# Block transposes on VectorE and DMAs in place of TensorE transposes for z, x1 and the attention's output

## The chip, the cores and the metric

The kernel runs on one core of one Trainium2 chip. The metric is the device time of one execution in microseconds (us). TensorE (PE) multiplies, VectorE (DVE), ScalarE (ACT) and GpSimd (POOL) do the element-wise work, and SyncE (SP) issues all the DMAs. Each engine works through its own queue in the order in which the program hands it instructions; engines wait for one another through semaphores.

## The reference

Two branches read the same normalised input, and their sum is added to x. There are S = 2048 tokens with D = 576 features; all data are float32.

```python
x = A_x
xn = _layernorm(x, axis=-1)
return x + _A_ref(xn, A_wqkv, A_wo) + _B_ref(xn, B_w1, B_w2, B_w3, B_w4)
# _A_ref: qkv = xn @ wqkv; 32 heads of 18; each token attends to 8 tokens, 2 apart, behind it
#         softmax over the 8; o = attn . v; return o @ wo
# _B_ref: z = layernorm(xn); h = gelu(z @ w1); four quarters of h shifted by +1, -1, +2, -2 tokens
#         x1 = xn + shifted @ w2
#         return x1 + gelu(layernorm(x1) @ w3) @ w4        # w3: 576 x 4608, w4: 4608 x 576
```

## The kernel before

Every product is made of float32r halves: an operand is split into a rounded part ("hi") and the rest ("lo"), and the pairs hi.hi, hi.lo and lo.hi are added up in PSUM. 576 features are four chunks of 128 and one tail of 64; in the fifth chunk the hi part of the tail lies in partitions 0 to 63 and its lo part in 64 to 127, so one matmul treats both. With that there are 14 matmuls per product (`PAIRS`).

A matmul wants the features in the partitions, while the norms want the tokens there. So a normalised token tile (128 tokens x 576) is transposed: `transposes` (L97) lets TensorE transpose four 128x128 blocks into a PSUM buffer, and for every second tile a fifth block that holds the 64-wide tails of two tiles side by side (`tail_half`, `pair_tail`). ScalarE then copies the hi part out of PSUM (L107, L110) and VectorE subtracts it for the lo part (L111, L114). The result goes into a block of 512 tokens, `xt[128, 9, 512]`, in a ring of two buffers (`ring_block`).

The stages, one after the other on TensorE:

- **QKV** (to L348): 16 token tiles; `x_stage` normalises and transposes xn two tiles ahead, `q_half` multiplies it by half of wqkv, and `spill` writes the result to DRAM.
- **Mix** (L422 on): four blocks b of 512 tokens. For each, `mix_tile` (14 matmuls with 512 columns into one of `psa`'s two PSUM buffers, two gelus on ScalarE, one subtraction on VectorE) for m = 0, 1, 2, then `mix_rem` (9 matmuls; its result goes through eight DMAs L400/L401 and a list of later steps, `todo`), then `mix_tile` 3. `z_norm` and `z_prep` prepare the z tiles of the next block, one after each of the first four. Between them the four or five pieces of w2 are loaded (`load_w2`, two buffers; piece 4 has eight DMAs, L370) and split.
- **W2** (L481 on): 16 token tiles; `mm_tok` writes one of `psb`'s three PSUM buffers, VectorE adds it to Y and takes the statistics for the next norm; from tile 6 on, `n_norm` and `n_prep` prepare x1 tile t - 6.
- **MLP units** (L697 on): 72 units (c, b), c = 0 to 17 and b = 0 to 3. A unit has two `up` (14 matmuls with 512 columns, two gelus, one subtraction) and then the four `down` of the unit before it (12 matmuls each, one addition to Y on VectorE). `LATE` names the x1 tiles 8 to 15, which are prepared in units 0 to 2. From unit 3 on, VectorE gets the attention in small pieces between its other work (`bg`); the attention's DMAs are on SP as well, and its result goes to DRAM (`od`). Weights w3 and w4 are loaded by `load_f` into `rawf`, which has two buffers; so is wo (`load_wo`, L660) in the last four units.
- **Output** (L750 on): 16 token tiles of o, loaded from `od` (`load_o`), transposed by `prep_o` three tiles ahead, multiplied by wo and added to Y; VectorE also adds x again (L695). Then the tile is stored.

The schedule is written by hand: the order of the calls is the order in each engine's queue. A tile of a pool is reused when whatever used its memory before has been released.

Of the kernel before, what the change touches and what calls it, by code (L numbers as in the profile page):

```python
# [8 lines left out]
F32 = mybir.dt.float32  # L9
# [20 lines left out]
HF = D // 2  # L30
# [15 lines left out]
def fused_block(ctx, tc, x, wqkv, wo, w1, w2, w3, w4, out):  # L46
# [25 lines left out]
    def tail_half(t):  # L72
        if t % 2 == 0:
            ztail[t // 2] = base.tile([128, 128], F32, name="ztail", bufs=2)
        return ztail[t // 2][:, t % 2 * 64:t % 2 * 64 + 64]

    def norm_z(dst, kind, t):
        norm(dst, Y[:, t, :512], kind, t)
        norm(tail_half(t), Y[:, t, 512:], kind, t)
# [36 lines left out]

    def split_w(dst_hi, dst_lo, raw):
        act.copy(dst_hi, raw)  # L118
        dve.tensor_tensor(dst_lo, raw, dst_hi.bitcast(F32), op=ALU.subtract)
# [20 lines left out]
    zp = {}  # L140

    def z_norm(t):
        zp[t] = w1pool.tile([128, 512], F32, name="z", bufs=2)
        norm_z(zp[t], 1, t)

    def z_prep(t):
        xt = ring_block(("z", t // 4))
        transposes(zp[t], pair_tail(ztail[t // 2], xt, t), xt, (t % 4) * 128)
# [177 lines left out]
    for t in range(4, NT):  # L326
        for h in range(2):
            q_half(t, h)
            if h == 0:
# [6 lines left out]
                if t >= NT - 2:  # L336
                    z_prep(2 * (t - NT + 2) + 1)
                    z_norm(2 * (t - NT + 2) + 3)
                if t in (5, 6):
                    split_w1(t - 5)  # L340
            else:
                if t == NT - 4:
                    z_norm(0)
                    z_norm(1)
                if NT - 3 <= t < NT - 1:
                    z_prep(2 * (t - NT + 3))
                    z_norm(2 * (t - NT + 3) + 2)
# [13 lines left out]
    pool.memset(T4[:, S:S + 4].bitcast(F32), 0.0)  # L361

    def load_w2(k):
        r = mpool.tile([128, D], F32, name="rz", tag="rz", bufs=2)
# [11 lines left out]
    def mix_tile(b, m):  # L376
        xt = xring[("z", b)]
        ps = psa.tile([128, 512], F32, name="p1", tag="a")
        for i, (a, w) in enumerate(PAIRS):
            pe.matmul(ps, W1[:, w, m * 128:(m + 1) * 128], xt[:, a, :],  # L380
                      start=i == 0, stop=i == len(PAIRS) - 1)
        g32 = mpool.tile([128, 512], F32, name="g32", bufs=1)
# [8 lines left out]
    def mix_rem(b):  # L391
        xt = xring[("z", b)]
        ps = psa.tile([128, 512], F32, name="p1", tag="a")
        for a in range(9):
            pe.matmul(ps, W1R[:, a if a < 5 else a - 5, :], xt[:, a, :], start=a == 0, stop=a == 8)  # L395
        u = mpool.tile([128, 512], F32, name="u", bufs=2)
        v = mpool.tile([128, 512], F32, name="v", bufs=2)
# [24 lines left out]
    for b in range(NB):  # L422
        for i, m in enumerate((0, 1, 2, 4, 3)):
            nz = 4 * (b + 1) + i
# [44 lines left out]
    def n_norm(t, zpool):  # L469
        zp[t] = zpool.tile([128, D], F32, name="rz", tag="rz", bufs=2)[:, :512]  # L470
        norm_z(zp[t], 2, t)

    def n_prep(t):
        xt = x1n.get(t // 4)
        if xt is None:
            xt = x1n[t // 4] = ring_block(("n", t // 4))
        transposes(zp[t], pair_tail(ztail[t // 2], xt, t), xt, (t % 4) * 128)
# [3 lines left out]
    for t in range(NT):  # L481
        ps = psb.tile([128, 2, 512], F32, name="ps", tag="b")
        if 6 <= t < 14:
            n_norm(t - 6, mpool)
# [12 lines left out]
        if t in (1, 3):  # L497
# [14 lines left out]
    hp = ctx.enter_context(tc.tile_pool(name="hp", bufs=2, reuse_waits="tile"))  # L512

# [98 lines left out]
    def up(c, b, i):  # L612
        f = c * C + i
        ps = psa.tile([128, 512], F32, name="p1", tag="a")
        for n, (a, w) in enumerate(PAIRS):
            pe.matmul(ps, W3[f][:, w, :], x1n[b][:, a, :], start=n == 0, stop=n == len(PAIRS) - 1)  # L616
# [28 lines left out]
    LATE = {(0, 0): (8, 9), (0, 1): (10, 11), (1, 0): (12,), (1, 1): (13,), (2, 0): (14,), (2, 1): (15,)}  # L645
    Wo = None
    oT = {}
# [27 lines left out]
    def load_o(t):  # L675
        if t % 2 == 0 and t < NT:
# [119 lines left out]
```

## Time and profile before

| what | us |
|---|---|
| median of 3 runs | 1322.92 |
| lowest and highest run | 1322.52, 1323.04 |
| the profiled execution | 1322.94 |
| span of its instructions | 1321.2 |
| TensorE, matmuls busy | 1312.1 (99%) |
| VectorE busy | 921.9 (70%) |
| ScalarE busy | 348.2 (26%) |
| mean granted TensorE clock | 1.0 |

In the profiled execution the mix begins at 197 us, the W2 stage at 264, the units at about 328 and the output at 1250. Busy time of an engine is a mean over stages, and a matmul's duration overlaps the next one's; so the chain of work that ended last, and the starts in the timeline, say more of TensorE's pace than its busy share. In rows of the groups, "out<-in" are the program's names, then come the shapes, the count, the busy time and the mean duration in ns, and at the end the idle time before the group with what released it. Rows with "SPq" are SP's queue; their time includes waits when several are merged.

### The profile page before, as it was taken

The numbers are of one execution on the slowest core, as the hardware profiler recorded it, in microseconds if no ns is written. First come the engines' busy times: TensorE is split into PE (matmuls) and PEld (weight loads), VectorE is DVE, ScalarE is ACT, GpSimd is POOL, SyncE is SP. The second block draws the span as 40 slices with busy tenths as digits, with TensorE's granted clock in tenths as the row PEclk, the third lists the DMA queues.
The fourth block names the chain that finished last, engine by engine and source line by source line (L and its number), as shares of the span: only waits on it lengthen the run. The fifth ranks groups of instructions, "written<-read, shape, count | busy, mean of one in ns | idle before, by whom it ended". The sixth has DMA issues, their size and how long they took to land.

```text
span 1321.2 us, 18855 instructions
## 1 busy us (share of the span) xinstructions
PE 1312.1 (99%) x7894; PEld 1208.0 (91%) x7894; DVE 921.9 (70%) x1332; ACT 348.2 (26%) x633; POOL 35.2 (3%) x92
## 2 busy tenths in 40 slices
PE   8999999999999999999999999999999999999998
PEld 8999998899899999999999999999999999999998
DVE  6443326687676778878868868878877886884454
ACT  4322225411423222222122222223213223122111
POOL 2010100011000000000000000000000000000000
PEclk9999999999999999999999999999999999999999
DMA  7644322020112021221221220220320200212164
GB/s 211 152 107 108 98 68 69 18 82 28 59 30 80 20 71 39 71 71 39 71 71 29 80 71 20 90 71 20 90 71 19 82 28 20 71 42 95 46 192 140
DMA packets 120325, 93.76 MB, mean 71 GB/s; under 512 B 73504, under 2 KB 100000, under 8 KB 120240
## 3 DMA queue, kind: packets, MB, share of 16 engines
q1 hardware_dynamic: 120240, 92.56, 23.9%
q8 instruction: 62, 1.02, 0.3%
q14 instruction: 23, 0.19, 0.0%
HBM read 67.83 MB, written 23.66 MB: 69 GB/s over the span
## 4 chain that ended last, share of the span: by engine, by line
PE 96%; DVE 2%; ACT 1%; SPq 1%; issue 1%; DMA 0%; POOL 0%; DVEq 0%; ACTq 0%; POOLq 0%
PE ps L636 34%; PE p L616 34%; PE ps L133 18%; PE ps L230 3%; PE p L380 3%; PE ps L102 2%; PE p L272 0%; PE p L395 0%; PE p L764 0%; DVE bn L88 0%; PE ps L105 0%; ACT xt L107 0%; DVE xt L111 0%; SPq L370 0%; DVE xt L114 0%
## 5 line engine op out<-in xcount | busy, mean ns | idle before, releaser
L636 PE MATMUL ps<-W,hi 128*128 128x288 f32 x2304 | 397.9, 294 | 0.5 <-DVE oT L114 0.5
L636 PEld LDWEIGHTS ps<-W,hi 128*128 128x128 f32 x2304 | 339.5, 188 | 6.1 <-PE ps L102 0.7
L620 ACT ACTIVATE hi<-p 128x512 fp32r<-128x512 f32 x144 | 86.2, 599 | 619.3 <-PE p L616 619.3
L636 PE MATMUL ps<-W,lo 128*128 128x288 f32 x1152 | 245.3, 294 | 0.0
L616 PE MATMUL p<-xt,W 128*128 128x512 f32 x1008 | 235.4, 390 | 0.0
L616 PE MATMUL p<-x1n,W 128*128 128x512 f32 x1008 | 234.9, 389 | 0.0
L622 DVE TENSOR_TENSOR lo<-g,hi 128x512 fp32r<-128x512 f32 x144 | 99.7, 692 | 193.2 <-ACT g L621 193.2
L639 DVE TENSOR_TENSOR Y<-ps,Y 128x576 f32<-128x576 f32 x288 | 212.8, 751 | 16.3 <-PE ps L636 16.1
L616 PEld LDWEIGHTS p<-x1n,W 128*128 128x128 f32 x1008 | 187.2, 188 | 36.8
L616 PEld LDWEIGHTS p<-xt,W 128*128 128x128 f32 x1008 | 187.1, 188 | 36.9
L636 PEld LDWEIGHTS ps<-W,lo 128*128 128x128 f32 x1152 | 185.4, 187 | 0.0
L133 PE MATMUL ps<-WQ,xt 128*128 128x432 f32 x672 | 135.3, 360 | 0.0
L133 PEld LDWEIGHTS ps<-WQ,xt 128*128 128x128 f32 x672 | 125.2, 188 | 5.2
L111 DVE TENSOR_TENSOR xt<-ps,xt 128x512 fp32r<-128x512 f32 x40 | 27.6, 689 | 87.2 <-ACT xt L110 52.1
L568 DVE TENSOR_TENSOR prod<-q,k 128x1152 f32<-128x1152 f32 x64 | 86.5, 1351 | 0.0
L571 DVE TENSOR_REDUCE L<-prod 128x64 f32<-128x1152 f32 x64 | 86.2, 1347 | 0.0
L621 ACT ACTIVATE g<-p 128x512 f32<-128x512 f32 x144 | 85.4, 593 | 0.0
L548 DVE TENSOR_TENSOR prod<-v,L 128x1152 f32<-128x1152 f32 x56 | 75.6, 1350 | 0.0
L552 DVE TENSOR_TENSOR o<-o,prod 128x1152 f32<-128x1152 f32 x56 | 75.6, 1350 | 0.0
L118 ACT CAST W<-rawf 128x640 fp32r<-128x640 f32 x72 | 50.5, 702 | 68.9 <-PE ps L636 62.2
L133 PE MATMUL ps<-Wo,oT 128*128 128x288 f32 x420 | 59.1, 298 | 0.2
L133 PEld LDWEIGHTS ps<-Wo,oT 128*128 128x128 f32 x420 | 56.2, 188 | 1.4 <-issue 1.4
(103 smaller groups left out, 941.9 us busy)
## 6 DMA issues: line engine op xcount, KB each, us to landing
qkvd<-stg SPq DMA_DIRECT2D x24, 432.0 KB, 3.4
rawf<-in_B_w_dram SPq DMA_DIRECT2D x36, 288.0 KB, 3.0
rawf<-in_B_w_dram SPq DMA_DIRECT2D x36, 256.0 KB, 2.9
xin<-in_A_x_dram SPq DMA_DIRECT2D x16, 288.0 KB, 3.8
q<-qkvd SPq DMA_DIRECT2D x8, 576.0 KB, 3.8
k<-qkvd SPq DMA_DIRECT2D x8, 576.0 KB, 5.7
v<-qkvd SPq DMA_DIRECT2D x8, 576.0 KB, 5.9
od<-o SPq DMA_DIRECT2D x8, 576.0 KB, 4.9
```

Of the source, the lines that this page charges most:

```text
L118: act.copy(dst_hi, raw)
L133: pe.matmul(ps[:, h, :n], xs(a), ws(b, h), start=i == 0, stop=i == len(PAIRS) - 1)
L548: dve.tensor_tensor(dst, vv, Lf[:, :, w:w + 1].to_broadcast([128, TPP * GH, HD]), op=ALU.mult)
L552: dve.tensor_tensor(o, o, dst, op=ALU.add)
L568: dve.tensor_tensor(prod.rearrange("p (j h) d -> p j (h d)", h=GH), q, k[:, r0:r0 + TPP, :], op=ALU.mult)
L571: dve.tensor_reduce(Lf[:, :, w], prod, axis=AX.X, op=ALU.add)
L616: pe.matmul(ps, W3[f][:, w, :], x1n[b][:, a, :], start=n == 0, stop=n == len(PAIRS) - 1)
L620: act.activation(hi, ps, AF.Gelu_apprx_tanh)
L621: act.activation(g32, ps, AF.Gelu_apprx_tanh)
L622: dve.tensor_tensor(lo, g32, hi.bitcast(F32), op=ALU.subtract)
L636: pe.matmul(ps[:, k, :HF], h[:, col], w[:, p, k * HF:(k + 1) * HF], start=n == 0, stop=n == len(seq) - 1)
L639: dve.tensor_tensor(yv, ps[:, :, :HF], yv, op=ALU.add)
```

## The change

z, x1 and o are no longer transposed by TensorE; xn still is. A normalised tile is turned by VectorE in 32x32 blocks (`turn`): each group of 32 partitions turns its own blocks, so a feature lands in the right place within its group of 32, but in the group of its tokens. Four tiles go into one staging tile ST; then `move` issues sixteen DMAs, one for each pair of token group q and feature group r, which carry the blocks to the partitions where they belong. They land as raw float32 in `xt[:, 4:9]`, and `split_x` makes the hi and lo parts of a whole block of 512 tokens at once: three copies on ScalarE, two subtractions on VectorE. ST has a single buffer in each stage.

Within a block the tokens then lie in the order (q, tile, 32) in place of (tile, q, 32). Matmuls that read z or x1 as the moving operand read them through `in_order`, 16 runs of 32 columns; o is loaded from DRAM in an order (`quads`) that makes up for it.

The order of the calls changes with it: in QKV, tiles of z are turned at t = 11, 12 (block 0, moved at t = 13, split at t = 14) and t = 14, 15 (block 1, moved at the end). In the mix, block b + 1 is moved at the start of b, split after its first `mix_tile`, and block b + 2 is turned after the four others. In the W2 stage, x1 tile t - 6 is turned at tile t, moves stand at t = 9 and 13, splits at 11 and 15. Tiles 8 to 11 are turned in unit 0 and 12 to 15 in unit 1. o is loaded in blocks of four tiles into one buffer; blocks 0 and 1 are turned in units 69 and 70 and split in 70 and 71, blocks 2 and 3 in the output stage at tiles 0 to 7, with moves at 3 and 7 and splits at 5 and 9.

```diff
+    def turn(st, src, t):
+        c = slice(32 * t, 32 * t + 32)
+        dve.transpose(st[:, 4:20, c], src[:, :512].rearrange("p (j c) -> p j c", c=32))
+        dve.transpose(st[:, 0:4, c].rearrange("p (a j) c -> p a j c", a=2),
+                      src[:, 512:].rearrange("p (j c) -> p j c", c=32)[:, None, :, :]
+                      .to_broadcast([128, 2, 2, 32]))
+
+    def move(st, xt):
+        for q in range(4):
+            for r in range(4):
+                sp.dma_start(xt[32 * r:32 * r + 32, 4:9, 128 * q:128 * q + 128].bitcast(F32),
+                             st[32 * q:32 * q + 32].rearrange("p (k r) c -> p k r c", r=4)[:, :, r, :])
+
+    def split_x(xt, rt):
+        raw = xt.bitcast(F32)
+        act.copy(rt[64:128, :], raw[64:128, 4, :])
+        act.copy(xt[0:64, 4, :], raw[0:64, 4, :])
+        act.copy(xt[:, 0:4, :], raw[:, 5:9, :])
+        dve.tensor_tensor(xt[64:128, 4, :], raw[64:128, 4, :], rt[64:128, :].bitcast(F32),
+                          op=ALU.subtract)
+        dve.tensor_tensor(xt[:, 5:9, :], raw[:, 5:9, :], raw[:, 0:4, :], op=ALU.subtract)
+
+    def in_order(blk):
+        return blk.rearrange("p (q t c) -> p t q c", q=4, t=4)
+
+    def quads(t_, b, q):
+        return dram_ap(t_, (512 * b + 128 * q) * D, [[D, 32], [32 * D, 4], [1, D]])
...
-                if t >= NT - 2:
-                    z_prep(2 * (t - NT + 2) + 1)
-                    z_norm(2 * (t - NT + 2) + 3)
+                if t == 13:
+                    move(ST, ring_block(("z", 0)))
...
+                if t == 14:
+                    split_x(xring["z", 0], RT)
+            if t in (11, 12):
+                z_turn(2 * (t - 11) + h)
+            if t in (14, 15):
+                z_turn(4 + 2 * (t - 14) + h)
+    move(ST, ring_block(("z", 1)))
...
-            pe.matmul(ps, W1[:, w, m * 128:(m + 1) * 128], xt[:, a, :],
+            pe.matmul(ps, W1[:, w, m * 128:(m + 1) * 128], in_order(xt[:, a, :]),
...
     for b in range(NB):
+        if 0 < b < NB - 1:
+            move(ST, ring_block(("z", b + 1)))
         for i, m in enumerate((0, 1, 2, 4, 3)):
...
-            if b + 1 < NB and i < 4:
-                z_prep(nz)
-                if nz + 2 < NT:
-                    z_norm(nz + 2)
+            if b + 1 < NB and i == 0:
+                split_x(xring["z", b + 1], RT)
+            if b + 2 < NB and i > 0:
+                z_turn(4 * (b + 2) + i - 1)
...
+    def n_turn(t, zpool, st):
+        z = zpool.tile([128, D], F32, name="rz", tag="rz")
+        norm(z, Y[:, t, :], 2, t)
+        turn(st, z, t % 4)
...
+        if t < 5:
+            while len(todo) > 4 - t:
+                todo.pop(0)()
...
         if 6 <= t < 14:
-            n_prep(t - 6)
-        if 2 <= t and todo:
-            todo.pop(0)()
+            n_turn(t - 6, rzpool, nst)
+        if t in (9, 13):
+            x1n[t // 4 - 2] = ring_block(("n", t // 4 - 2))
+            move(nst, x1n[t // 4 - 2])
+        if t in (11, 15):
+            split_x(x1n[t // 4 - 2], nrt)
...
-            pe.matmul(ps, W3[f][:, w, :], x1n[b][:, a, :], start=n == 0, stop=n == len(PAIRS) - 1)
+            pe.matmul(ps, W3[f][:, w, :], in_order(x1n[b][:, a, :]), start=n == 0, stop=n == len(PAIRS) - 1)
...
-    LATE = {(0, 0): (8, 9), (0, 1): (10, 11), (1, 0): (12,), (1, 1): (13,), (2, 0): (14,), (2, 1): (15,)}
+    LATE = {(0, 0): (8, 9, 10, 11), (1, 0): (12, 13), (1, 1): (14, 15)}
...
+    def load_o(b):
+        if b < NB:
+            otile[b] = opool.tile([128, 4, D], F32, name="ot", bufs=1)
+            for q in range(4):
+                sp.dma_start(otile[b][32 * q:32 * q + 32], quads(od, b, q))
...
+    def o_turn(b, tiles):
+        for t in tiles:
+            turn(ST2, otile[b][:, t, :], t)
...
             load_wo(0)
             load_wo(2)
+            load_o(0)
         if u == NU - 3:
             split_wo(0)
             load_wo(4)
-            load_o(0)
-            load_o(2)
             load_xa(0)
             load_xa(1)
+            o_turn(0, range(4))
+            move(ST2, ring_block(("o", 0)))
+            load_o(1)
         if u == NU - 2:
             split_wo(2)
+            split_x(xring["o", 0], RT2)
+            o_turn(1, range(4))
+            move(ST2, ring_block(("o", 1)))
+            load_o(2)
         if u == NU - 1:
             split_wo(4)
+            split_x(xring["o", 1], RT2)
         for i in range(C):
             bg(r, False)
-            ts = LATE.get((u, i), ())
-            for t in ts:
-                n_norm(t, hp)
             up(c, b, i)
-            for t in ts:
-                n_prep(t)
+            for t in LATE.get((u, i), ()):
+                n_turn(t, tp, ST2)
+                if t in (11, 15):
+                    move(ST2, x1n[t // 4])
...
+        if u in (0, 1):
+            split_x(x1n[2 + u], RT2)
...
     for t in range(NT):
+        b, s = divmod(t, 4)
...
+        if b + 2 < NB:
+            o_turn(b + 2, (s,))
+            if s == 3:
+                move(ST2, ring_block(("o", b + 2)))
+                load_o(b + 3)
+        if 1 <= b < 3 and s == 1:
+            split_x(xring["o", b + 1], RT2)
```

More of the change, by code (lines that the diff above doesn't have):

```diff
@@ L394, in mix_rem @@
         for a in range(9):
[L395 to L397 removed]
+            pe.matmul(ps, W1R[:, a if a < 5 else a - 5, :], in_order(xt[:, a, :]), start=a == 0, stop=a == 8)
+        u = mupool.tile([128, 512], F32, name="u", bufs=2)
+        v = mupool.tile([128, 512], F32, name="v", bufs=2)
         act.copy(u, ps)
```

87 lines of the change are left out of this document (34 added, 53 removed).

## The prediction

> **What bounds the kernel now.** I read the page first: busy time of each engine, then the chain that ended last.
>
> ```profile
> PE 1312.1 (99%) x7894; PEld 1208.0 (91%) x7894; DVE 921.9 (70%) x1332; ACT 348.2 (26%) x633; POOL 35.2 (3%) x92
> PE 96%; DVE 2%; ACT 1%; SPq 1%; issue 1%; DMA 0%; POOL 0%; DVEq 0%; ACTq 0%; POOLq 0%
> ```
>
> TensorE is 96% of the chain, so time leaves this kernel only where TensorE does less, and comes back wherever TensorE is made to wait. What it does at full pace stands in the chain in order of time (start, length, what):
>
> ```profile
> 167.57 5.47 PE ps L133 x28
> 196.96 3.20 PE p L380 x14
> 208.04 2.09 PE p L395 x9
> 264.08 26.00 PE ps L133 x196
> 378.14 6.36 PE p L616 x28
> 384.50 6.34 PE ps L636 x48
> 1293.56 3.95 PE ps L133 x28
> 1302.24 3.96 PE ps L133 x28
> 1306.75 7.45 PE ps L133 x56
> ```
>
> A `q_half` is 5.5 us, a `mix_tile` 3.2, `mix_rem` 2.1, a token tile against W2 or Wo 3.72 (26.00/196 x 28), an `up` 3.18, a `down` 1.59. The last three rows price the transposes: two output tiles with their nine transposes take 1302.24 - 1293.56 = 8.68 us, the last two, which have none beside them, 7.45; so 0.62 us a tile.
>
> The rest of the argument is about queues, so the waits come next (engine and line, what was waited for: us in total, times, longest), then SP's own timeline and the landings of its DMAs.
>
> ```profile
> ACT v L406 <- DVE u L405: 15.4, 4, 8.5
> PE p L380 <- ACT g L386: 0.8, 2, 0.4
> ```
>
> The first row shows ScalarE standing before one instruction for up to 8.5 us: its queue runs in program order, and the gelu behind must wait too. The second shows that TensorE waits when a gelu has not emptied one of `psa`'s two buffers. There is little of it now; both rows matter below.
>
> ```profile
> 198.40 1.72 SPq L366 DMA_DIRECT2D rz<-in_B_w_dram  x2
> 217.08 3.76 SPq L370 DMA_DIRECT2D rz<-in_B_w_dram  x8
> 246.80 0.51 SPq L400 DMA_DIRECT2D v<-u  x1
> 247.35 0.59 SPq L401 DMA_DIRECT2D v<-u  x1
> ...
> 251.15 0.59 SPq L401 DMA_DIRECT2D v<-u  x1
> 1185.33 20.29 SPq L663 DMA_DIRECT2D rawf<-in_A_wo_dram  x2
> ```
> ```profile
> v<-u SPq DMA_DIRECT2D x32, 32.0 KB, 2.0
> ot<-od SPq DMA_DIRECT2D x8, 512.0 KB, 4.3
> ```
>
> Eight small SBUF-to-SBUF DMAs in a row leave SP 0.62 us apart ((251.15 - 246.80)/7) and each lands 2.0 us after its issue.
>
> **The change, part by part.**
>
> *Removed.* Transposes of 16 tiles each of z, x1 and o: 48 x 0.62 = **-30 us**, all on TensorE's path.
>
> *The move.* Sixteen DMAs on SP, 80 KB each, per 512 tokens. Nearest row is `v<-u` (same queue, SBUF to SBUF): 15 x 0.62 + 2.0 and 0.2 for the larger size = **11.5 us from first issue to landed**, called L. Bounds: 15 x 0.47 + 2.0 = 9.1 by the L370 row (3.76/8); 15 x 0.86 + 4.3 = 17.2 if each issues like L366's two (1.72/2) and lands like the far larger `ot`. I take 11.5, since that row moves between the same memories. The Trainium skill (SBUF — State Buffer, "Door 1: The DMA port swizzle") gives 189 GB/s for 32 partitions; an estimate from it is 1.31 MB/189 GB/s = 6.9 us plus the landing, 8.9 us, and with that alone the sum below would be some 29 us less. The rows speak for the issue as the tighter limit.
>
> *turn and split_x.* Durations of their nearest groups (busy, mean ns):
>
> ```profile
> L387 DVE TENSOR_TENSOR h<-g,h 128x512 fp32r<-128x512 f32 x16 | 11.1, 693 | 25.3 <-ACT g L386 25.1
> L94 DVE TENSOR_SCALAR Y<-xin,mv,rs 128x576 f32<-128x576 f32 x16 | 9.3, 578 | 6.5 <-POOL rs L91 6.4
> L114 DVE TENSOR_TENSOR oT<-ps,oT 64x128 fp32r<-64x128 f32 x16 | 4.6, 289 | 0.3
> L119 DVE TENSOR_TENSOR WQ<-raw,WQ 128x1296 fp32r<-128x1296 f32 x2 | 3.0, 1508 | 6.7 <-ACT WQ L118 6.7
> L119 DVE TENSOR_TENSOR WQ<-raw,WQ 128x288 fp32r<-128x288 f32 x5 | 2.0, 453 | 0.0
> L118 ACT CAST WQ<-raw 128x1296 fp32r<-128x1296 f32 x2 | 2.6, 1278 | 0.0
> L118 ACT CAST WQ<-raw 128x288 fp32r<-128x288 f32 x5 | 2.0, 431 | 4.8 <-DMA raw<-in_A_wqkv_dram 4.8
> L398 ACT COPY u<-p 128x512 f32<-128x512 f32 x4 | 2.4, 602 | 0.9 <-PE p L395 0.9
> L385 ACT ACTIVATE h<-p 128x512 fp32r<-128x512 f32 x16 | 9.6, 598 | 23.7 <-PE p L380 23.7
> L495 DVE TENSOR_TENSOR Y<-ps,Y 128x576 f32<-128x576 f32 x16 | 12.1, 758 | 9.6 <-PE ps L133 9.2
> L88 DVE BATCH_NORM_STATS2 bn<-Y 128x6 f32<-128x288 f32 x64 | 26.2, 451 | 0.7
> L89 DVE BATCH_NORM_AGGREGATE mv<-bn 128x2 f32<-128x12 f32 x48 | 10.0, 209 | 1.6
> L90 DVE TENSOR_SCALAR rs<-mv 128x1 f32<-128x1 f32 x48 | 7.4, 154 | 1.7
> L405 DVE TENSOR_TENSOR u<-u,v 128x512 f32<-128x512 f32 x4 | 2.7, 685 | 0.0
> L406 ACT ACTIVATE v<-u 128x512 fp32r<-128x512 f32 x4 | 2.5, 632 | 15.4 <-DVE u L405 15.4
> L414 DVE SCALAR_TENSOR_TENSOR T<-v,sgn,u 32x512 fp32r<-32x512 f32 x16 | 11.9, 746 | 0.6
> L119 DVE TENSOR_TENSOR W<-rz,W 128x576 fp32r<-128x576 f32 x5 | 3.8, 756 | 0.1
> ```
>
> No row has a VectorE transpose. Its 512 and 128 elements I price as one element a step, like L387 and L114: 0.69 + 0.29 = 0.98 us a tile. Lower bound 0.75 (L94's rate for the long part); upper bound four times as long for four-byte data, 3.9. With its norm a tile costs 1.56. `split_x` on ScalarE: two copies at 0.60 and one of 128x2048, by the slope between 288 and 1296 columns (0.84 ns each) 1.91: **3.1 us**. Behind it VectorE's subtraction of 2048 (1.047 ns each): **2.3 us**. A gelu pair is 1.2; add plus statistics on VectorE 2.0 (0.76 + 2 x 0.45 + 0.21 + 0.15).
>
> *`in_order`.* The moving operand of 2276 matmuls (2016 `up`, 224 + 36 in the mix) is read in 16 runs of 32. No row has such a read. Lower bound 0; upper bound, each run paying a matmul's fixed part: 227 ns for 512 columns and 132 for 288 give 0.42 ns a column and 10 ns fixed, so 15 x 10 = 150 ns each. I take 0, as nearly all of a matmul's time is per column.
>
> *Where the moves are waited for.* `split_x` stands in ScalarE's and VectorE's queues ahead of gelus and adds that empty PSUM, and each move must wait for its four turns, which stand behind the previous `split_x`. The clocks below walk this (us).
>
> The move of z0 is the covered one: it starts when the first half of token tile 13 has been copied out, needs 11.5 us, and its `split_x` stands behind the copy of tile 14's second half, three halves or 16.5 us on. Without that cover it would stall like the next.
>
> Mix, 0 = TensorE done with QKV. Move of z1 starts at 1.5 (L366's start, right behind the last spill, against 196.96), landed 13.0, ScalarE free 16.1, gelu of tile 1 done 17.3; TensorE, through with tiles 0 to 2 at 9.6, waits until then. Block 0 ends 22.9 (pace: 14.9). VectorE finishes the four turns at 28.2, W2's third split at 29.0; SP is at `v<-u` until 29.8, then L370's eight DMAs take until 33.6, and only then the move of z2: landed 45.1, gelu 1 done 49.4; the next gelu also waits for `todo`'s add (L405) and its gelus, so block 1 ends at 59.2. Its turns end at 64.1; move of z3 landed 75.6, block 2 ends 88.1, block 3 at 103.0. Pace alone is 4 x 14.9 = 59.6: **stall 43.4**.
>
> x1, 0 = TensorE done with W2 tile 9. Move of n0 at 3.6, landed 15.1. `turn(4)` overwrites ST and waits for it, with tile 11's add behind; tiles 14 and 15 find no PSUM buffer and start at 16.9 and 23.5; TensorE ends at 27.2 (pace 22.3). Move of n1 at 29.9, landed 41.4, ScalarE free 44.5, x1n[1] complete 46.8. Unit 0's gelus wait for that; unit 1's first `up` starts at 46.8. Four turns (8 to 11) end at 53.7, landed 65.2; the gelus of unit 1 and, behind them, four more turns keep VectorE until 78.2, so the fourth `down` of unit 0 waits (57.6 pass three of them, 79.0 frees a buffer). The move of x1n[3] lands at 89.7; the adds of unit 1's `down`s stand behind its split; unit 2 ends at 99.2 instead of 54.1: **stall 45.1**.
>
> o, 0 = start of unit 69. `load_o(0)` now stands on SP behind `load_wo(2)`, which was issued 1205.6 (20.29 us row) where unit 69 began at 1203.7, and lands at 7.8; VectorE waits there with four adds behind, turns until 11.7; move landed 23.3, `load_o(1)` 27.5, second move 32.8 to 44.3. Units 69 to 71 lose 3, 8 and 4 us. In the output loop `load_o(3)` lands 16 us after its move began and `turn` waits for it; tile 7 starts 5 us late, and o3, landed 39 us after tile 3 started, holds tile 12 until 47.7 instead of 33.5. **Stall 29.6**.
>
> Between unit 3 and unit 68 nothing is changed. SP's other work behind the moves has slack: the attention's five loads, issued in unit 1, are needed in unit 3.
>
> *Sum.* 1322.9 - 30 + 43.4 + 45.1 + 29.6 = **1411 us**, from the profiled execution's 1322.94 (span 1321.2 and 1.7 around it; the median of three is 1322.92).
>
> L enters 11 times in a row (3, 4 and 4): **11 us for each us of L**.
>
> **The rivals.**
>
> *The moves are there before they are asked for* (the other side). Then only the -30 counts: 1293. It decides from L = 3.6 us, where the stalls are down to 30 (118 - 11 x 7.9). For it: L is 2.0 for one DMA. Against: sixteen issues of 0.62.
>
> *SP issues quicker*, 0.47 as L370: L = 9.1, 11 x 2.4 = 26 less: 1385. For: those rows; against: they read from DRAM.
>
> *VectorE's transpose is slow*: 32 of the 48 turns lie on the chains (8, 12, 12); at +2.1 each 1478. No row speaks.
>
> *`in_order` costs TensorE*: 10 ns on 2276 matmuls is 23: 1434.
>
> *A cold TensorE.* Rows of its timeline:
>
> ```profile
> 1.37 5.38 PE L272 MATMUL p<-ident 128*128 128x128 f32 x24 [1.37 <-POOL ident masks.py:199]
> ```
> ```profile
> 331.57 1.04 PE L102 MATMUL ps<-ident,rz 128*128 128x128 f32 x8
> ```
>
> The first transposes take 224 ns each, later ones 130: 2.3 us lost after the idle start. Some nine stalls above 4 us would cost at most 21: 1432; I leave it out of the sum, as much of it would vanish in the next wait for a move. The Trainium skill (TensorE: Matmul & The Clock Gate, "What's actually happening") has the clock halved after an idle window and restored after a busy one; no long pause within this trace tests that.
>
> **How the numbers follow.** Forecast 0.52, quicker issue 0.17, cold TensorE 0.14, slow transpose 0.08, `in_order` 0.05, moves in time 0.04. The range 1355 to 1475 takes in the first three with 25 us below the quicker issue and 43 above the cold one for errors of the walk, and leaves out most of the rest. This kernel's times can tell 0.2% from no change. Faster 0.03 and same 0.01 are the moves in time, either side of L = 3.6; slower 0.96.
>
> **What would show it.** Sixteen DMAs of a move some 10 us long on SP; ScalarE and VectorE idle before `split_x`, released by DMA; TensorE idle in slices of the mix (three gaps), at the start of the units, and after unit 69; `up` matmuls still 227 ns apart; no transposes of z, rz and ot. I am wrong if TensorE's idle time stays under 30 us, or if the moves land within 4 us.

## The result, and the profile after

The kernel after takes 1446.04 us (median of 4 runs, 1443.15 to 1446.45) against 1322.77 for the kernel before (4 runs, 1322.52 to 1323.04): a ratio of 1.0927, interval 1.091 to 1.0943. It is slower by 123.3 us; the forecast was 1411, the range 1355 to 1475.

First the page of the kernel after: busy time of each engine, then the chain that ended last.

```profile
PE 1328.4 (92%) x7678; PEld 1207.0 (84%) x7678; DVE 942.9 (65%) x1324; ACT 346.3 (24%) x573; POOL 36.1 (2%) x92
PE 79%; SPq 8%; DVE 5%; DMA 3%; ACT 2%; issue 2%; ACTq 0%; DVEq 0%
```

TensorE has 216 instructions fewer (7894 to 7678) and is busy 16.3 us longer. Its share of the chain fell from 96% to 79%; SP's queue, 1% before, now holds 8%, and DMA landings 3%. The work that the change took from TensorE did leave it; what came in is time in which it waits, or runs slowly: its idle time, span less busy, rose from 9.1 to 116.1 us. The windows of the kernel after say where (stretch; then for each engine busy us and instructions; the granted clock; the DMA engines' share; GB/s).

```profile
194.00:270.00 76.00, 47.69 (x176) 36.82 (x175) 29.55 (x48) 22.23 (x34) 0.75 (x18) 0.80 0.37 80
...
345.00:442.00 97.00, 57.72 (x302) 51.23 (x302) 46.97 (x83) 19.12 (x26) 5.12 (x14) 0.79 0.34 82
442.00:1294.00 852.00, 852.00 (x5019) 767.34 (x5018) 657.91 (x758) 209.58 (x355) 0.00 (x0) 1.00 0.17 54
```

TensorE is idle 28.3 of 76 us in the first row (blocks 0 to 2 of the mix) and 39.3 of 97 in the second shown (the end of W2's stage and the first units), and the mean granted clock of these stretches is 0.80 and 0.79; between 442 and 1294 it never stops and the clock is full. The borders of the stages stand in the chains (start, length, what): two rows of the kernel before, then those of the kernel after.

```profile
365.36 2.72 PE p L616 x12
1203.74 2.28 PE p L616 x10
```
```profile
194.87 0.89 ACT stg L265
301.75 1.33 PE ps L160 x10
442.25 2.13 PE p L656 x5
1291.96 2.13 PE ps L676 x16
```

In the second block, the first row is where the chain leaves TensorE, done with QKV, for ScalarE's copy; the last ends at 1294.09, where unit 69 begins. With 196.96 and 264.08 from the prediction's chain, and the spans 1321.2 and 1444.5, each stage's length gives a ledger, beside what the prediction's steps come to for the same stage (its stalls less 0.62 us for each transpose that left):

| stage | before | after | difference | forecast |
|---|---|---|---|---|
| to the end of QKV | 197.0 | 194.9 | -2.1 | -2.5 |
| the mix | 67.1 | 106.9 | +39.8 | +36.0 |
| W2 and units 0 to 2 | 101.3 | 140.5 | +39.2 | +35.2 |
| units 3 to 68 | 838.4 | 851.8 | +13.5 | 0 |
| unit 69 to the end | 117.5 | 150.4 | +32.9 | +19.7 |
| sum | 1321.2 | 1444.5 | +123.3 | +88.4 |

The mix shows the mechanism. Three views of the kernel after, for the same stretch: SP's timeline (start, length, instruction), the landings in the chain that ended last, and TensorE's timeline (in brackets how long it sat idle before and what released it).

```profile
196.24 11.01 SPq L126 DMA_DIRECT2D xt<-ST  x16
...
228.98 10.67 SPq L126 DMA_DIRECT2D xt<-ST  x16
...
261.15 10.34 SPq L126 DMA_DIRECT2D xt<-ST  x16
```
```profile
206.65 2.14 DMA xt<-ST
...
239.05 2.17 DMA xt<-ST
```
```profile
212.94 3.93 PE L424 MATMUL p<-xt,W1R 128*128 128x512 f32 x9 [8.35 <-ACT g L415]
...
245.46 4.21 PE L424 MATMUL p<-xt,W1R 128*128 128x512 f32 x9 [15.52 <-ACT g L415]
251.71 15.89 PE L409 MATMUL p<-xt,W 128*128 128x512 f32 x56 [2.05 <-ACT g L415]
277.28 4.16 PE L424 MATMUL p<-xt,W1R 128*128 128x512 f32 x9 [9.68 <-ACT g L415]
```

The z1 move starts at 196.24, all sixteen DMAs are issued at 207.25, and the last lands at 208.79: 12.55 us; the z2 move, 228.98 to 241.22, takes 12.24. Only then does ScalarE's queue move on, its gelu frees a PSUM buffer, and TensorE starts. (From first issue to last landing, the eleven moves behind z0's, which is the covered one, average 12.1 us in this trace.) TensorE's own release is named as the gelu; the waits (total us, times, longest; TensorE's four largest) show what the gelu's engine stood for:

```profile
ACT RT L131 <- DMA xt<-ST: 203.9, 9, 41.7
PE ps L676 <- DVE Y L679: 39.5, 5, 19.5
PE p L424 <- ACT g L415: 33.5, 3, 15.5
PE ps L160 <- DVE Y L812: 16.9, 2, 10.1
PE p L656 <- ACT g L661: 11.6, 1, 11.6
```

The first row is `split_x` of z, o and half of x1 (two more such waits, 40.1 us, stand under the name x1n); the other four are TensorE, 101.5 us in eleven waits. Not all of the first row costs time: 203.9 us is what ScalarE stood there, much of it with nothing else to do.

### The profile page after: what moved, and what is told of

Its sections match the earlier page's. It is cut to its first block, busy times and chain, and to the rows that moved or that the text cites. A ratio compares the mean times of both kernels' runs of the same rounds, so it can differ in the third digit from the quotient of the medians.

```text
span 1444.5 us, 18621 instructions
## 1 busy us (share of the span) xinstructions
PE 1328.4 (92%) x7678; PEld 1207.0 (84%) x7678; DVE 942.9 (65%) x1324; ACT 346.3 (24%) x573; POOL 36.1 (2%) x92
## 4 chain that ended last, share of the span: by engine, by line
PE 79%; SPq 8%; DVE 5%; DMA 3%; ACT 2%; issue 2%; ACTq 0%; DVEq 0%
PE ps L676 30%; PE p L656 30%; PE ps L160 14%; SPq L126 7%; PE ps L255 3%; PE p L409 2%; DMA ot<-od 1%; DVE ST L118 1%; DMA xt<-ST 1%; DVE xt L136 1%; ACT xt L133 1%; DVE rz L90 0%; PE ps L98 0%; PE p L424 0%; DVE ST L119 0%
## 5 line engine op out<-in xcount | busy, mean ns | idle before, releaser
L676 PE MATMUL ps<-W,hi 128*128 128x288 f32 x2304 | 404.2, 297 | 39.5 <-DVE Y L679 39.5
L676 PEld LDWEIGHTS ps<-W,hi 128*128 128x128 f32 x2304 | 346.1, 190 | 47.4 <-DVE Y L679 40.6
L656 PE MATMUL p<-xt,W 128*128 128x512 f32 x1008 | 243.9, 399 | 11.8 <-ACT g L661 11.6
L676 PE MATMUL ps<-W,lo 128*128 128x288 f32 x1152 | 248.9, 297 | 0.0
L656 PE MATMUL p<-x1n,W 128*128 128x512 f32 x1008 | 244.6, 400 | 0.0
L656 PEld LDWEIGHTS p<-xt,W 128*128 128x128 f32 x1008 | 188.9, 190 | 55.8 <-ACT g L661 12.1
L656 PEld LDWEIGHTS p<-x1n,W 128*128 128x128 f32 x1008 | 190.4, 191 | 43.4
L160 PE MATMUL ps<-Wo,xt 128*128 128x288 f32 x420 | 59.3, 304 | 16.9 <-DVE Y L812 16.9
L160 PEld LDWEIGHTS ps<-Wo,xt 128*128 128x128 f32 x420 | 58.8, 197 | 17.4 <-DVE Y L812 10.3
L409 PE MATMUL p<-xt,W 128*128 128x512 f32 x224 | 55.9, 410 | 3.6 <-ACT g L415 3.6
```

The source lines that it names most:

```text
L160: pe.matmul(ps[:, h, :n], xs(a), ws(b, h), start=i == 0, stop=i == len(PAIRS) - 1)
L409: pe.matmul(ps, W1[:, w, m * 128:(m + 1) * 128], in_order(xt[:, a, :]), start=i == 0, stop=i == len(PAIRS) - 1)
L656: pe.matmul(ps, W3[f][:, w, :], in_order(x1n[b][:, a, :]), start=n == 0, stop=n == len(PAIRS) - 1)
L676: pe.matmul(ps[:, k, :HF], h[:, col], w[:, p, k * HF:(k + 1) * HF], start=n == 0, stop=n == len(seq) - 1)
```

## The experiments

What stood to be told apart: theory A, that the time is the move's length L (issue on SP plus landing) through the queues behind `split_x`; and, as rivals for the part the forecast missed, the strided read, a cold TensorE, and late loads of o.

### Strided reads removed

```diff
     def in_order(blk):
-        return blk.rearrange("p (q t c) -> p t q c", q=4, t=4)
+        return blk
```

> The changed kernel with one edit: the 2276 matmuls read z and x1 contiguously, without in_order, so the tokens of a block stay in the order of the moves (the shifts and the sums then pair other tokens). In the changed kernel's trace a pair of up takes 6.53 us where it took 6.36 before, 6.3 ns a matmul. Theory A (the read in 16 runs costs 6.3 ns each): 2276 x 6.3 = 14 us less, 1432 us, and a pair of up back at 6.36. Theory B (the slower up comes from the clock after the long waits, not from the read): no change, 1446 us, up still 6.53 in the middle units.

Measured: 1432.9 us (1431.64 to 1433.76), ratio 1.0832 (1.0816 to 1.0848), 13.1 less than the kernel after. The chains at the start of the steady stretch: first the kernel after, then this run; the first row of each is unit 3's `up` pair, behind a wait.

```profile
442.25 7.89 PE p L656 x28
...
456.57 6.53 PE p L656 x28
```
```profile
441.01 7.84 PE p L656 x28
...
455.29 6.35 PE p L656 x28
```

An `up` pair takes 6.53 us with the strided read and 6.36 without, as before the change: 0.17/28 = 6 ns a matmul. By the two medians, all 2276 together cost 13.1 us. The 66 units from 3 to 68, for which the forecast had nothing, hold 66 x 0.17 = 11.2 of it. Unit 3's pair, 7.89, is 1.4 us longer than those behind it, but so it is in this run (7.84): that part is not the read. The granted clock was 0.50 there (439 to 445 us of the kernel after).

### Fewer and more DMAs in a move

Four DMAs, each over all 128 partitions:

```diff
         for q in range(4):
-            for r in range(4):
-                sp.dma_start(xt[32 * r:32 * r + 32, 4:9, 128 * q:128 * q + 128].bitcast(F32),
-                             st[32 * q:32 * q + 32].rearrange("p (k r) c -> p k r c", r=4)[:, :, r, :])
+            sp.dma_start(xt[:, 4:9, 128 * q:128 * q + 128].bitcast(F32),
+                         st.rearrange("p (k r) c -> p k r c", r=4)[:, :, q, :])
```

> Each move is four DMAs over all 128 partitions in place of sixteen over 32: the same bytes in the same 512-byte pieces, but the blocks stay in their quadrants, so z, x1 and o are multiplied with other features than the reference. Theory A (the time is SP's issue of the DMAs, and ScalarE and VectorE stand before the split until the last has landed): first issue to landed falls from 12 us to 3 x 0.64 + 3.1 = 5 us, seven us less at eleven places, 77 us less and some of the cold matmuls with it: 1350 to 1375 us. Rival (the bytes or the 512-byte pieces take the time): landed after 12 us as before, 1440 to 1446. Rival (turns and splits on VectorE are the limit): at most 20 us less.

Thirty-two DMAs, each of the sixteen in two pieces:

```diff
             for r in range(4):
-                sp.dma_start(xt[32 * r:32 * r + 32, 4:9, 128 * q:128 * q + 128].bitcast(F32),
-                             st[32 * q:32 * q + 32].rearrange("p (k r) c -> p k r c", r=4)[:, :, r, :])
+                for k0, k1 in ((0, 3), (3, 5)):
+                    sp.dma_start(xt[32 * r:32 * r + 32, 4 + k0:4 + k1, 128 * q:128 * q + 128].bitcast(F32),
+                                 st[32 * q:32 * q + 32].rearrange("p (k r) c -> p k r c", r=4)[:, k0:k1, r, :])
```

> Each move is 32 DMAs in place of sixteen (three and two of the five chunks), same bytes, same result. Theory A: first issue to landed 31 x 0.645 + 2.2 = 22 us, ten more at eleven places: 110 us more, 1556 (1535 to 1570). Rival (bytes): at most 10 us more.

Measured: four DMAs 1391.22 us (1386.27 to 1393.62), ratio 1.0513 (1.049 to 1.0535); thirty-two 1555.12 (1552.55 to 1555.54), ratio 1.1752 (1.1735 to 1.177). SP's timeline and the landing in the chain, for the move of z2, first with four DMAs, then with thirty-two:

```profile
224.54 3.22 SPq L125 DMA_DIRECT2D xt<-ST  x4
```
```profile
226.68 4.24 DMA xt<-ST
```
```profile
242.39 20.50 SPq L127 DMA_DIRECT2D xt<-ST  x32
```
```profile
262.30 1.90 DMA xt<-ST
```

For this move L is 226.68 + 4.24 - 224.54 = 6.4 us with four and 21.8 with thirty-two; over the eleven moves it averages 7.6 and 22.1 in the two traces, against 12.1 in the kernel after. The times follow: 54.8 us less for 4.5 less of L, 109.1 more for 10.0 more. That is 12.1 and 10.9 us for each us of L; the forecast had 11. The bytes and their 512-byte pieces are the same in all three, so what sets L is above all the number of DMAs: 0.64 to 0.69 us each on SP (20.50/32, 11.01/16), and 0.80 for the four larger ones (3.22/4). Only the run with thirty-two changes the number alone; the four also span four times the partitions. They land in 4.2 us where the sixteen land in 2.2, and in up to 8.6 in the last stage: with L = 7.6 for the expected 5, this run missed its time.

The Trainium skill (SBUF — State Buffer, "Door 1: The DMA port swizzle") would have the sixteen bounded by the bandwidth of 32 partitions, 189 GB/s; by that the estimate of L was 8.9. The trace doesn't show that limit at work: with twice the DMAs of half the size the landing behind the last issue stays at 1.90 us, and the issue alone takes 20.5.

### TensorE kept busy while it waits

Work whose result nobody reads, placed before `mix_rem` of blocks 0 to 2; first 50, 100 and 60 transposes of the identity, then 37, 67 and 43 matmuls of 512 columns:

```diff
             else:
+                fill = (50, 100, 60, 0)[b]
+                if fill:
+                    keep = psb.tile([128, 2, 512], F32, name="ps", tag="b")
+                    for _ in range(fill):
+                        pe.transpose(keep[:, 0, :128], ident, ident)
                 todo += mix_rem(b)
```

> In the mix TensorE does 50, 100 and 60 transposes of the identity, read by nobody, before mix_rem of blocks 0, 1 and 2, where it waits 8.4, 15.5 and 9.7 us now. Theory A (TensorE is slow for some us after a long wait): mix_rem falls from 3.9 to 4.2 us to 2.1 to 2.3, the granted clock of the mix from 0.80 to above 0.95, the time by 2 to 7 us (block 1's end is set by VectorE, so not all three gains arrive): 1439 to 1444. Rival (mix_rem is slow for another reason, its operands or its read): mix_rem stays at 4 us and the time at 1446 or above.

Measured: 1449.81 us (1447.28 to 1452.97), ratio 1.0954 (1.0936 to 1.0972). The transposes took 112 ns each and left 3.7, 5.6 and 3.1 us of idle time before `mix_rem`, whose nine matmuls still took 3.65 to 4.07 us. This run did not test what it was to test.

```diff
+                fill = (37, 67, 43, 0)[b]
...
+                    for n in range(fill):
+                        pe.matmul(keep[:, 0, :], W1[:, 0, 0:128], xring[("z", b)][:, 0, :],
+                                  start=n == 0, stop=n == fill - 1)
```

> As the run with transposes before mix_rem, which left TensorE idle for its last 3 to 6 us and mix_rem at 3.7 to 4.1 us, but with 37, 67 and 43 matmuls of 512 columns, which fill the waits of 8.4, 15.5 and 9.7 us to their ends; nobody reads them. Theory A (TensorE is slow after an idle stretch): mix_rem of blocks 0, 1 and 2 falls to 2.1 to 2.4 us, the matmuls in the filled stretch run at 227 to 235 ns throughout, and the time falls by 2 to 7 us to 1439 to 1444. Rival (mix_rem is slow for its own sake): mix_rem stays near 4 us, the time at 1446 or above.

Measured: 1447.1 us (1444.99 to 1451.03), ratio 1.0943 (1.0925 to 1.0962). TensorE's timeline of this run, beside the rows of the kernel after shown above:

```profile
214.24 2.37 PE L424 MATMUL p<-xt,W1R 128*128 128x512 f32 x9 [0.66 <-ACT g L415]
...
247.40 2.37 PE L424 MATMUL p<-xt,W1R 128*128 128x512 f32 x9 [2.01 <-ACT g L415]
253.65 16.15 PE L409 MATMUL p<-xt,W 128*128 128x512 f32 x56 [3.88 <-ACT g L415]
```

The windows of the second `mix_rem`, first in the kernel after, then in this run (the granted clock is the third figure from the end):

```profile
245.46:249.50 4.04, 4.04 (x9) 2.80 (x9) 3.87 (x6) 0.10 (x1) 0.00 (x0) 0.50 0.00 0
```
```profile
247.40:249.70 2.30, 2.30 (x9) 1.61 (x9) 2.30 (x3) 0.00 (x0) 0.00 (x0) 1.00 0.00 0
```

With the idle time filled, `mix_rem` takes 2.37 us where it takes 3.93 and 4.21 after an idle 8.35 and 15.52: TensorE is slow after a wait, and loses 1.6 to 1.8 us on these nine matmuls. The Trainium skill (TensorE: Matmul & The Clock Gate, "What's actually happening") says that the clock is halved after an idle window; the granted clock of 0.50 behind the wait, and of 1.00 where there was none, agrees. But the time did not fall: behind `mix_rem` TensorE again stands, 3.88 us in the third row where the kernel after has 2.05, for the same queue of ScalarE. A faster `mix_rem` only reaches the next wait sooner. What the cold clock costs in the other stages wasn't tried.

### Two queues

```diff
             for r in range(4):
-                sp.dma_start(
+                (sp if q < 2 else act).dma_start(
                     xt[32 * r:32 * r + 32, 4:9, 128 * q:128 * q + 128].bitcast(F32),
```

> Eight of each move's sixteen DMAs are issued by ScalarE in place of SyncE, at the same place of the program. Theory A (the issue, 0.645 us each on one queue, is what is long): the two queues issue side by side, first issue to landed 7 x 0.645 + 2.2 = 6.7 us, five less at eleven places; ScalarE has 5 us of issue more at each, most of it while it would wait anyway: 1390 to 1405 us. Rival (both queues share what makes the descriptors, or the DMA engines are the limit): landed after 12 us as before, and with ScalarE's added issue 1446 to 1460.

Measured: 1418.82 us (1415.47 to 1420.32), ratio 1.0725 (1.0706 to 1.0743): 27 less than the kernel after, and 14 above the upper end of what was expected. First the move of z2 on ScalarE's queue and the gelu behind it, then a later move on both queues, by the timelines of ScalarE and SP:

```profile
219.88 5.23 ACTq L126 DMA_DIRECT2D xt<-ST  x8
225.16 0.60 ACT L415 ACTIVATE h<-p 128x512 fp32r<-128x512 f32 x1 [7.58 <-DMA xt<-ST]
```
```profile
1352.07 5.55 ACTq L126 DMA_DIRECT2D xt<-ST  x8
...
1352.11 5.97 SPq L126 DMA_DIRECT2D xt<-ST  x8
```

The two queues do issue side by side, but eight DMAs then take 5.55 and 5.97 us here, and 6.4 to 8.8 at four of the eleven moves, against 5.2 for SP's eight of z2's move, which were issued alone. The median landing grows from 2.2 to 3.1 us. And those eight of z2's move begin only at 226.92, behind other DMAs on SP, so that this move takes 13.8 us. Over the eleven moves L averages 9.7 us, not the expected 6.7: 2.4 less than in the kernel after, which at 11 us for each us is 26 of the 27 us won. ScalarE's eight stand ahead of its gelus (the gelu at 225.16 starts when the last is out, and TensorE waits 3.87 us for it); by this sum that cost little on balance, but it was not measured by itself.

### The same moves, asked for later

Sixteen DMAs on SP as in the kernel after, but each move starts as early as its turns allow, and each `split_x` and turn stands as late in the queues of ScalarE and VectorE as its reader allows. A second staging tile holds x1's tiles 12 to 15, and the attention runs one unit later. The core of it, for the mix:

```diff
-            if b + 1 < NB and i == 0:
-                split_x(xring["z", b + 1], RT)
-            if b + 2 < NB and i > 0:
-                z_turn(4 * (b + 2) + i - 1)
+            if i == 3:
+                if b + 2 < NB:
+                    for j in range(4):
+                        z_turn(4 * (b + 2) + j)
+                if b + 1 < NB:
+                    split_x(xring["z", b + 1], RT)
...
-        if t in (11, 15):
-            split_x(x1n[t // 4 - 2], nrt)
+        if t == 13:
+            split_x(x1n[0], nrt)
...
+        if u == NU - 4:
+            o_turn(0, range(4))
+            load_o(1)
+            move(ST2[0], ring_block(("o", 0)))
```

> The same sixteen DMAs on SyncE per move, all parts of the change kept, but moves issued earlier and splits and turns put later in the queues, so that few gelus and adds stand behind a move in flight: in the mix turns and split of the next block after mix_rem; x1 tiles 0 to 7 turned at tiles 4, 5, 10, 11 of the W2 stage, 8 to 15 at the start of unit 0 into two staging tiles, split after units 1 and 2; the attention starts one unit later; o loaded before the last wo piece, turned and split at the ends of units 68 to 71 and in the output stage. Theory A (the time lies in what is queued behind a move in flight): idle TensorE falls from some 110 us to 45, the time to 1365 to 1390. Rival (the added work of VectorE, ScalarE and the matmuls' read are the cost): at most 20 us less.

Measured: 1383.04 us (1381.85 to 1384.44), ratio 1.0456 (1.044 to 1.0472): 63 less than the kernel after with no DMA changed. SP's and TensorE's timelines of this run:

```profile
216.84 10.63 SPq L126 DMA_DIRECT2D xt<-ST  x16
```
```profile
214.10 1.22 PE L408 MATMUL p<-xt,W 128*128 128x512 f32 x2 [4.12 <-ACT xt L133]
219.87 10.88 PE L408 MATMUL p<-xt,W 128*128 128x512 f32 x40 [4.55 <-DVE xt L136]
...
243.98 12.32 PE L408 MATMUL p<-xt,W 128*128 128x512 f32 x40 [6.62 <-DVE xt L136]
```

The move issues for 10.6 us as ever, yet z2's starts at 216.84 instead of 228.98, and TensorE now waits for the split itself (4.12 and 4.55, then 6.62) instead of for a gelu stuck behind it (8.35, 15.52 and 9.68). TensorE's idle time falls from 116.1 to 58.8 us. So some 63 of the 123 us came from where the moves and their waits stand in the queues, with the second staging tile that this order needs; its parts were not tried one by one. The largest wait left is 9.41 us, before the fourth `down` of unit 69: its PSUM buffer is freed by an add that stands behind the split of o's first block, and the attention, which runs a unit later here, hands o over late.

### Later, and on two queues

The order of the run above with the two queues of the one before it.

> The late order with each move's DMAs half on SyncE and half on ScalarE. Theory A: moves land after 7 us, most of them covered: idle TensorE near 20 us, the time 1325 to 1350, no better than the kernel before by much, as in_order keeps 14 us of the 30 that the transposes took. Rival as for the late order alone.

Measured: 1391.03 us (1390.89 to 1392.54), ratio 1.0519 (1.0503 to 1.0534): a miss, 8 slower than with one queue. The moves did not get as short as expected: L averages 11.1 us over the eleven moves, against 12.5 with the late order alone and the 7 expected, since at four of them SP's half begins 4.3 to 7.1 us after ScalarE's (L is 11.3 to 15.8 there; the others take 8.7 to 10.6). The landing is 3.4 us on ScalarE's queue and 3.2 on SP's, and ScalarE's issues of 5.2 to 7.4 us again stand ahead of gelus. So this run doesn't tell what a move of 7 us would be worth in the late order.

### Later, with the high part in token order

```diff
-        act.copy(xt[:, 0:4, :], raw[:, 5:9, :])
+        for k in range(4):
+            act.copy(xt[:, k, :].rearrange("p (t q c) -> p t q c", q=4, t=4), in_order(raw[:, 5 + k, :]))
...
-        dve.tensor_tensor(xt[:, 5:9, :], raw[:, 5:9, :], raw[:, 0:4, :], op=ALU.subtract)
+        for k in range(4):
+            dve.tensor_tensor(in_order(xt[:, 5 + k, :]), in_order(raw[:, 5 + k, :]),
+                              raw[:, k, :].rearrange("p (t q c) -> p t q c", q=4, t=4), op=ALU.subtract)
```

> Changed against e7_late: split_x writes the rounded high part in the token order itself (four copies of 512 columns, read in 16 runs of 32, and four subtractions likewise), so 8 of an up's 14 matmuls read 512 columns in one run and 6 still read 16 runs of 32. The result is the same as that of the kernel after. Theory A (each read in runs costs a matmul 6.3 ns, so 8 of 14 times 2276 matmuls get it back): 8 us less than e7_late's 1383, 1373 to 1377, if the copies take no longer than before. Rival (the copies and subtractions in runs of 32 take longer, and each split_x stands in queues that TensorE waits for): what the matmuls gain is given back, 1380 to 1388.

Measured: 1369.79 us (1368.53 to 1370.64), ratio 1.0354 (1.0339 to 1.037), the best of these runs: 13.3 less than with the late order alone and below the expected 1373 to 1377. But not by the expected way. Its chain, and its groups of the split on ScalarE and VectorE (busy, mean ns; idle before):

```profile
402.08 6.52 PE p L671 x28
```
```profile
L144 DVE TENSOR_TENSOR xt<-xt 128x512 fp32r<-128x512 f32 x24 | 15.0, 687 | 1.1 <-ACT xt L137 0.9
L137 ACT CAST xt<-xt 128x512 fp32r<-128x512 f32 x24 | 13.1, 615 | 0.0
```

An `up` pair takes 6.52 us, 0.01 less than with every read strided, though 8 of each 14 matmuls now read 512 columns in one run. From start to start, averaged over 54 such pairs of the trace, the first two matmuls, both read in one run, take 227 ns each; behind the first strided one, matmuls of both kinds take 229 to 240. So the read's price doesn't go by the count of strided matmuls; what it goes by stays open. The gain is ahead of the steady stretch: the first `down`s behind the last wait of the early units start at 382.88 here and at 396.51 with the late order alone, by the chains of the two (this run first):

```profile
382.88 6.34 PE ps L691 x48
```
```profile
396.51 6.35 PE ps L682 x48
```
The split now comes in pieces of 512 columns (0.615 and 0.687 us), and the first matmuls can start on the first of them; that this is what saves the 13 us is argued from these rows, not tried by itself.

### One wide load of o

```diff
-            for q in range(4):
-                sp.dma_start(otile[b][32 * q:32 * q + 32], quads(od, b, q))
+            sp.dma_start(otile[b], od[512 * b:512 * (b + 1), :].rearrange("(t p) d -> p t d", t=4))
```

> Changed against the kernel after: load_o fetches the block's 512 rows with one DMA over 128 partitions (each partition gets four whole rows of 2304 bytes), where the kernel after has four DMAs of 32 partitions each; the bytes and the pieces are the same. The tokens of a block of o come out in another order than the residual they are added to, so the output is not the reference's. Theory A (the narrow loads land late, 8.2, 6.2 and 6.7 us on the chain where 4.3 was taken, and four issues take 1.9 us where one takes 0.5): 8 us of landing and some 4 of issue leave the chain, 1433 to 1438 us. Rival (the landing is late because Wo's loads of 1.3 MB stand ahead of it in the DMA engines, and does not hang on the partitions): 6 to 8 us of landing stay, 1441 to 1447.

Measured: 1441.34 us (1439.62 to 1442.14), ratio 1.0892 (1.0874 to 1.0911): 4.7 less than the kernel after. The landings of o in the chain of the kernel after (each is the last of a block's four loads), then the first one of this run, and the loads of o in the list of DMA issues of the kernel after (count, KB each, median us to landing):

```profile
1297.45 8.19 DMA ot<-od
...
1321.21 6.17 DMA ot<-od
...
1388.26 6.66 DMA ot<-od
```
```profile
1295.88 6.90 DMA ot<-od
```
```profile
ot<-od SPq DMA_DIRECT2D x16, 288.0 KB, 5.5
```

The time is at the edge of the rival's range. One DMA over 128 partitions issues in 0.6 us instead of 1.85, and from first issue to landed the four blocks of o take 6.90, 5.62, 5.79 and 6.18 us where the narrow loads took 9.60, 7.77, 8.04 and 8.25. So the narrow loads cost 2 to 3 us a block, but most of the lateness stays without them. Nor do Wo's loads right ahead, the rival's cause, account for much: the kernel before had them right ahead of its first load of o, too, and that landed in 4.6 us. What the rows show instead is size. The 4.3 was the landing of a load of 512 KB; a block is now four of 288, 1152 KB, and the four of the first block land 5.5, 6.3, 7.3 and 8.2 us after their issues, one behind the other (the last block's 3.4, 4.7, 5.9 and 6.7; the 2 us between the two may be Wo's). That the bytes of a block set its landing is argued from these rows, not tried by itself.

## Why the prediction came out as it did

**Direction and mechanism: right.** The transposes left TensorE, and the moves came onto the path through the waits of `split_x` in ScalarE's and VectorE's queues. The rival that ends faster, moves in time, would have needed L = 3.6; L is 12.1, and even with four DMAs it is 7.6.

**Removed, -30.** The stage to the end of QKV, where four of the 48 go and no wait comes in, shortened by 2.1 (forecast 2.5). Of this 0.3 was there before any of the four: the chain's half that starts at 167.57 in the prediction starts at 167.28 here. So 0.45 us a tile, for 0.62.

**L = 11.5.** Measured 12.55, 12.24 and 11.9 in the mix, 12.1 over the eleven moves. The term from `v<-u` was nearly right (0.65 to 0.70 us from issue to issue for 0.62, 2.15 landing for 2.2): the quicker issue, 0.47, and the 17.2 of the other bound both fell. Times 11, the 0.6 us is 7 us, over the three stages with moves.

**11 us for each us of L: right.** 12.1 with four DMAs, 10.9 with thirty-two, 11.3 with two queues (27.2/2.4).

**turn and split_x: right.** Rows of the kernel after, the long part of the turns of x1 first, then the splits on ScalarE and VectorE:

```profile
L118 DVE STREAM_TRANSPOSE ST<-rz 128x512 f32<-128x512 f32 x16 | 11.4, 711 | 10.1 <-DMA xt<-ST 9.6
...
L133 ACT CAST xt<-xt 128x2048 fp32r<-128x2048 f32 x10 | 19.0, 1895 | 0.0
L136 DVE TENSOR_TENSOR xt<-xt 128x2048 fp32r<-128x2048 f32 x10 | 22.9, 2293 | 14.1 <-ACT xt L133 12.3 <-DMA ot<-od 1.8
```

A turn is 0.71 + 0.27 (its part of 128 columns) = 0.98 us, as forecast; the large copy 1.90 for 1.91; the large subtraction 2.29 for 2.3. The slow transpose is out.

**`in_order` = 0: the step that failed.** "I take 0, as nearly all of a matmul's time is per column": it costs 6 ns a matmul, within its bounds of 0 and 150, and over 2276 matmuls 13 of the 35 us that the forecast lacked. The sign that the prediction named, "`up` matmuls still 227 ns apart", failed: they are 233 apart. A term that small per instruction wasn't small, since it stood on TensorE's path in all 72 units; the rival that priced it at 10 ns was given 0.05.

**The mix and x1: 36.0 and 35.2 forecast, 39.8 and 39.2 measured.** The walk's clocks held: z2's move starts at 33.6 in the walk and at 228.98 - 194.8 = 34.2 in the trace, z3's at 64.1 and 66.4, block 3 ends at 103.0 and 106.9. The seven moves there took 4.6 us more than seven times 11.5, which is 5 of the 8 us; the strided reads of the mix and of units 0 to 2 give 2.

**o: 19.7 forecast, 32.9 measured.** "`load_o(0)` ... lands at 7.8" after unit 69 begins: it lands at 1297.45 + 8.19 - 1294.09 = 11.5. The landing was taken as 4.3 us from the loads of o before; on the chain it is 8.19, 6.17 and 6.66, 8 us more in all. This is the other term that was mis-sized: the row was of a load of 512 KB, and a block of four tiles is 1152 KB. 2 more come from L (11.9, 12.3, 11.8 and 12.0 for 11.5), and 3 of the 13 are not placed; the chain has slow matmuls there (60 of `down` in 10.78 us from 1350.69, 7.9 at full pace).

**A cold TensorE, left out: shown to be there, its price open outside the mix.** TensorE is busy 58 us at a granted clock of 0.50, all of it around the waits, so some 29 us longer than at full clock: an estimate, from the trace's record of the clock. In the mix, where it was tried, being warm gained nothing, as "much of it would vanish in the next wait for a move" has it. In the other stages it was not tried, and this rival, priced at 21 us, is not ruled out for a part of what the forecast lacked.

**Between unit 3 and unit 68 nothing is changed: wrong in the total**, by 13.5 us, 11.2 of them the strided read and 1.4 unit 3's slow start; no wait came in, and SP's other work behind the moves had its slack.

By terms, then: 13 us for the read, 7 for L, 8 for the landings of o, 1.4 for unit 3's slow start; the sum is 29 of 35, and some 6 are not placed, for which slow matmuls are the candidate. In the working of the range one sum is off: 1355 lies 30 us below the quicker issue's 1385, not 25.

## What to carry to other kernels

Replacing work of the bound engine by a chain of small DMAs trades its busy time for a delay, and the delay costs what stands behind the wait: price the issue count of the queue (here 0.64 to 0.70 us a DMA), then ask, for each engine whose queue holds the wait, which buffers it was going to free. Here sixteen DMAs of 80 KB a block cost more than the 30 us of transposes they replaced; a later order of moves and waits won 63 of the 123 us, and no order tried here got below 1369.79. A landing is best priced from a load of as many bytes. A change of a few ns in an instruction that runs 2000 times on the bound engine belongs in the sum, with a bound taken seriously.

## What the runs showed of the hardware that was not expected

- A matmul whose moving operand is read in 16 runs of 32 elements takes 6 ns more (6.53 for 6.36 us per 28); with 8 of 14 read in one run, nearly all of that remains (6.52), and only the two ahead of the first strided one take the old 227 ns.
- A DMA in a row on SP takes 0.64 to 0.69 us at 80 KB (10.34/16, 11.01/16), 0.64 at 48 and 32 KB (20.50/32), and 0.80 at 320 KB: issue goes by the count far more than by the bytes. Landing doubled from 2.2 to 4.2 us when four times the bytes were in each.
- Two queues issue side by side, but eight DMAs then take 5.6 and 6.0 us or more instead of 5.2, landings 3.1 us instead of 2.2, and a gelu behind eight issues on ScalarE's queue starts when the last is out.
- Behind waits of 15.52 and 9.68 us nine matmuls ran at a granted clock of 0.50 and took 4.21 and 4.16 us; with the wait filled, at 1.00, they took 2.37.
- Four loads of 288 KB in a row, of 32 partitions each, landed 5.5, 6.3, 7.3 and 8.2 us after their issues; one load of the same bytes over 128 partitions landed in 6.9.
- Identity transposes as filler (112 ns each) did not leave the nine matmuls behind them at full pace, 512-column matmuls did (2.37 us against 3.65 to 4.07); in the first case 3 to 6 us of idle time stood between, so whether the kind of work matters is open.
